# Loading q and k of two batches in token order, and transposing them by DMA

## The chip, the cores and the metric

The kernel runs on one core of a Trainium2 chip. A core has a matrix engine (TensorE, in the profile PE, its weight loads PEld), a vector engine (VectorE, DVE), a scalar engine (ScalarE, ACT), GpSimd (POOL) and SyncE (SP). GpSimd and SyncE only issue DMAs here: the loads from GpSimd, the stores and the DMA transposes from SyncE. The metric is device time of one execution in microseconds (us), lower is better. Three executions of the kernel before took 190.57, 191.4 and 191.51 us, median 191.4 us.

## The reference: what is computed

Attention with a local window of 96 keys and 8 global keys, over 4 batches, 8 heads, 768 tokens and a head dimension of 64, followed by a mixing block over 512 channels:

```python
scores = scale * np.matmul(q, k.transpose(0, 1, 3, 2))
keep = is_global | is_local            # first 8 keys, or 0 <= i - j < 96
scores = np.where(keep, scores + bias, -1e9)
x = softmax(scores) @ v                # then (B, S, 512)
theta = x @ w_theta
y = w_tok_r @ (x * cos(theta)) + w_tok_i @ (x * sin(theta))
u = x + y
out = u + np.maximum(u @ w_ch, 0.0)
```

q, k, v, the weights and the output are float32; the kernel casts its inputs to bfloat16 as they are loaded.

## The kernel before

Tokens are cut into `NT` = 6 tiles of 128, heads into `NP` = 4 pairs of two, so that a pair fills 128 rows (2 heads x 64).

**Loads.** `load_qk` (L69) and `load_v` (L76) issue from GpSimd. q and k come with six neighbouring tokens of a head on one partition, so one run in memory is 6 x 64 numbers (768 bytes as bfloat16). v comes in token order, so a run is 64 numbers (128 bytes). A batch from 1 on is loaded by `load_all` (L364): one DMA for q, one for k, one for v. The tile `qk` has one buffer: q and k of a batch can be loaded only when the last pair of the batch before has been read out of it. `vn` has two.

**Prep** (`prep`, L180), once per batch and pair. VectorE copies q and k of the pair into `qkn`, heads side by side (L189; for the first two pairs of batch 0, ScalarE copies k). TensorE transposes 6 tiles of q and 6 of k against the identity into PSUM (L198, 12 matmuls). VectorE copies q out as `qT` (L203) and ScalarE k as `kT` (L205); these copies also put the tokens back in order. Two VectorE copies build `kG` (L209, L210): the keys of the inner tiles, with the 8 global keys in place of the first 8 of each tile. `qT`, `kT` and `kG` have six buffers each, four of which a batch uses.

**Attention** (`scores` L215, `values` L262): per pair, three steps of score matmuls (L230), an exponential on ScalarE (L234) and a product with a table of biases on VectorE (L242, L245), then the matmuls with v (L278), a reciprocal and a product that give `x_sb` (L286, L288). `xtrans` (L290) transposes `x_sb` into `xT`, by DMA from batch 1 on (L292).

**Mixing**: `theta` (L304) multiplies by `w_theta` (L313), takes cosine and sine on ScalarE (L317, L318) and forms `zri` on VectorE (L321). `mix` (L326) holds the token matmuls (L332), and VectorE adds x to give `u` (L337). `utrans` (L341) transposes `u`, by DMA from batch 1 on (L346) but for the last tile. `chan` (L353) multiplies by `w_ch` (L357), VectorE forms the output tile (L360) and SyncE stores it (L362).

**Order.** Each batch has a head (the last channel matmuls of the batch before, the preps of the next batch and this batch's theta) and a mix phase, into which `weave` (L391) sets the attention of the next batch, step by step. `chan` follows `mix` by two tiles. In batch 0 the preps of batch 1 lie inside the mix phase; the preps of batches 2 and 3 lie in the heads of batches 1 and 2. TensorE's instructions keep the order of the program (`manual_schedule`, L409). On the other engines and on the DMA queues of GpSimd and SyncE a planner orders them when the program is built: among those that its own estimate of time holds to be ready, the earliest in the program first. So an instruction can be set ahead of earlier ones: the load of v for batch 2 stands in the program after those of q and k, but goes at 32.46 us, and q and k at 54.61 us. Where `behind` (L176) is used, an instruction can't be set ahead of the latest token matmul or the latest `u`; the copies into `qkn` and the TensorE transposes are held so. At run time each engine and each queue works strictly in the order it was given.

Of the kernel before, what the change touches and what calls it, by code (L numbers as in the profile page):

```python
# [10 lines left out]
BF = mybir.dt.bfloat16  # L11
# [5 lines left out]
def kernel(  # L17
# [13 lines left out]
    nc = tc.nc  # L31
    B, H, S, D = q.shape
    T = 128
    NT = S // T
    DM = H * D
    NC = DM // T
    NP = H // 2
    NG = int(n_global)
# [8 lines left out]
    ld = ctx.enter_context(tc.tile_pool(name="ld", bufs=2))  # L47
    att = ctx.enter_context(tc.tile_pool(name="att", bufs=2))
# [7 lines left out]
    def ps_small(shape, dtype):  # L56
        return small.tile(shape, dtype, name="ps", tag="ps")

    loads = {}

    def alloc_loads(b):
        qk = ld.tile([T, 2, H, NT, D], BF, name="qk", bufs=1)
        vn = ld.tile([T, H, NT, D + 1], BF, name="vn")
        nc.vector.memset(vn[:, :, :, D:D + 1], 1.0)
        loads[b] = (qk, vn)

    def load_qk(b, h0, n, which=(0, 1)):  # L69
        qk = loads[b][0]  # L70
        for i_ in which:
            nc.gpsimd.dma_start(  # L72
                out=qk[:, i_, h0:h0 + n].rearrange("p h t d -> p h (t d)"),
                in_=(q, k)[i_][b, h0:h0 + n].rearrange("h (p t) d -> p h (t d)", p=T))
# [5 lines left out]


    alloc_loads(0)
    load_qk(0, 0, 2)
    load_qk(0, 2, 2)
    load_v(0, 0, 4)
    load_qk(0, 4, 2)
    load_qk(0, 6, 2)
    load_v(0, 4, 4)
# [76 lines left out]
    def warm(n):  # L165
        ps = ps_small([T, 512], FP)
        for _ in range(n):
            nc.tensor.matmul(ps, lhsT=zero[:, 0:T], rhs=zero, start=True, stop=True)
# [3 lines left out]
    qkT = {}  # L172
# [3 lines left out]
    def behind(eng):  # L176

        return tc.issue_after(anchor[eng]) if eng in anchor else nullcontext()

    def prep(b, p, w=0):  # L180
        qk = loads[b][0]
        if (b, 0) not in qkT:
            x_sb[b] = moe.tile([T, NP, NT, T], BF, name="x_sb", bufs=2)
            xT_sb[b] = moe.tile([T, NC, S], BF, name="xT", bufs=1)

        qkn = att.tile([T, NT, 2, 2, D], BF, name="qkn", bufs=3)
        with behind("dve"):
            for i_ in range(2):
                (nc.scalar.copy if b == 0 and i_ and p < 2 else nc.vector.tensor_copy)(  # L189
                    out=qkn[:, :, i_].rearrange("p t h d -> p h t d"), in_=qk[:, i_, 2 * p:2 * p + 2])  # L190
        qT = att.tile([T, S], BF, name="qT", bufs=6)
        kT = att.tile([T, S], BF, name="kT", bufs=6)
        kG = att.tile([T, NT - 2, T], BF, name="kG", bufs=6)
        for i_, dst in ((0, qT), (1, kT)):
            ps = ps_small([T, NT, T], BF)
            with behind("pe"):
                for t_ in range(NT):
                    nc.tensor.transpose(ps[:, t_, :], qkn[:, t_, i_].rearrange("p h d -> p (h d)"), ident)  # L198

            dst = dst.rearrange("p (n t) -> p n t", t=NT)  # L200
            src = ps.rearrange("p t n -> p n t")
            if i_ == 0:
                nc.vector.tensor_copy(out=dst, in_=src)  # L203
            else:
                nc.scalar.copy(out=dst, in_=src)  # L205
            if w:
                warm(w)

        nc.vector.tensor_copy(out=kG, in_=kT[:, T:(NT - 1) * T].rearrange("p (t n) -> p t n", t=NT - 2))  # L209
        nc.vector.tensor_copy(out=kG[:, :, 0:NG], in_=kT[:, None, 0:NG].to_broadcast([T, NT - 2, NG]))  # L210
        qkT[(b, p)] = (qT, kT, kG)

    ebuf = {}
# [150 lines left out]
    def load_all(b):  # L364
        alloc_loads(b)
        load_qk(b, 0, 8)
        load_v(b, 0, 8)
# [41 lines left out]
    with tc.manual_schedule(engines={mybir.EngineType.PE}):  # L409
        warm(8)  # L410
        prep(0, 0, 4)
        distances()
        bias_table(0)
        for p in range(1, NP + 1):
            if p < NP:
                prep(0, p, 2 if p == 1 else 0)
                bias_table(p)
            if p == 2:
                vglob(0, 0, 4)
            if p == 3:  # L420
                vglob(0, 4, 4)
            for c in range(NT // 2):
                scores(0, p - 1, c)
                if p == 1:
                    warm(1)
            if p > 1:
                values(0, p - 2, 0)
                values(0, p - 2, 1)
            if p > 2:
                xtrans(0, p - 3, nc.scalar.copy)  # L430
        values(0, NP - 1, 0)
        values(0, NP - 1, 1)
        xtrans(0, NP - 2, nc.scalar.copy)
        xtrans(0, NP - 1, nc.scalar.copy)
        trans_w(0, nc.scalar.copy)
    rest = []
    for b in range(B):
# [3 lines left out]
        lag = 2  # L441
        th = [lambda c=c, j=j: theta(b, c, j) for c in range(NT // 2) for j in range(2)]
        pre = [lambda p=p: prep(nxt, p) for p in range(NP)] if nxt else []
        if b == 0:
            order = th
# [61 lines left out]
```

The softmax here doesn't subtract the row's maximum and nothing guards it: scores larger than these inputs give would overflow.

## Time and profile before

| | |
|---|---|
| median of three executions | 191.4 us |
| the profiled execution | 191.4 us |
| its span, first to last instruction | 189.6 us |
| mean granted TensorE clock | 0.973 |
| TensorE busy | 167.9 us, 89% |
| VectorE busy | 137.9 us, 73% |
| ScalarE busy | 102.9 us, 54% |
| packets of GpSimd's load queue | 35760 |
| packets of SyncE's queue | 22304 |

Busy times of TensorE overlap, since matmuls are pipelined and their ends are modelled: twelve transposes that follow each other have 0.22 us each in the profile, and the next group starts some 0.7 us after their first. So TensorE's cost is read from starts. Lines of the profile name a source line (L198), an engine, an operation, the tile written and the tiles read, how often, and then the busy time and the mean of one. Batches are numbered 0 to 3; "(2, 0)" is pair 0 of batch 2, and for `u` it is the tile of tokens.

### The profile page before, as it was taken

To read this page: it belongs to the slowest core of one execution; us is meant where nothing else is said; L and a number is where in the kernel's file an instruction comes from. 1 tells how busy PE (TensorE), PEld (TensorE's weight loads), DVE (VectorE), ACT (ScalarE), POOL (GpSimd) and SP (SyncE) were. 2 spreads that over 40 slices of the span, in tenths; PEclk is the share of its full clock that TensorE was granted. 3 is DMA by queue.
4 is the path that set the end of the run, shared out by engine and by line. 5 is a ranking of instruction groups with operands and counts; after the bars stand their busy time and mean duration, and the time that the engine had idled before them with its cause. 6 is when DMAs were issued, how large, how long until landed. Compare 5 with 4: busy or idle time off the path is not lost.

```text
span 189.6 us, 3693 instructions
## 1 busy us (share of the span) xinstructions
PE 167.9 (89%) x1500; PEld 89.1 (47%) x1523; DVE 137.9 (73%) x309; ACT 102.9 (54%) x122; POOL 27.1 (14%) x31
## 2 busy tenths in 40 slices
PE   7855787899999999999939999999999999999981
PEld 2424665445656555654414454644454544434430
DVE  5839987386999997998853786998877864734422
ACT  2469988871397684598724360499663604800010
POOL 7974361300040004020000000000000000000000
PEclk9999669999999999999987999999999999999999
DMA  4999999999999983999991337301165374113432
GB/s 63 153 188 181 210 209 207 204 189 142 130 83 182 225 116 75 148 142 146 223 116 58 74 91 185 109 3 55 28 66 141 88 145 148 59 32 107 118 106 111
DMA packets 58081, 23.97 MB, mean 126 GB/s; under 512 B 44240, under 2 KB 54992, under 8 KB 58064
## 3 DMA queue, kind: packets, MB, share of 16 engines
q0 software_dynamic: 35760, 12.85, 70.6%
q1 hardware_dynamic: 22304, 10.88, 25.0%
q8 instruction: 12, 0.20, 0.5%
q14 instruction: 5, 0.04, 0.1%
HBM read 25.69 MB, written 6.29 MB: 169 GB/s over the span
## 4 chain that ended last, share of the span: by engine, by line
PE 55%; ACT 14%; DVE 13%; DMA 12%; issue 2%; POOL 2%; ACTq 0%; POOLq 0%
PE ps L332 22%; PE ps L357 10%; DMA uT<-u 8%; PE pb L313 7%; ACT e L234 6%; PE pb L230 5%; DMA vn<-in_v_dram 4%; PE pb L278 4%; DVE qT L203 4%; ACT cs L317 3%; PE ps L198 3%; DVE qkn L189 2%; PE ps L278 2%; DVE zri L321 2%; POOL qk L72 2%
## 5 line engine op out<-in xcount | busy, mean ns | idle before, releaser
L234 ACT ACTIVATE e<-pb 128x1024 bf16<-128x1024 f32 (+1 forms) x48 | 44.1, 958 | 25.8 <-PE pb L230 25.7
L332 PE MATMUL ps<-zri,w_tokT_111 128*128 128x512 bf16 x141 | 53.6, 381 | 0.9 <-issue 0.3
L332 PE MATMUL ps<-zri,w_tokT_110 128*128 128x512 bf16 x130 | 49.5, 382 | 1.3 <-DVE zri L321 0.8
L337 DVE TENSOR_TENSOR u<-x_sb,ps 128x512 bf16<-128x512 bf16 x24 | 16.5, 687 | 16.6 <-PE ps L332 16.0
L357 PE MATMUL ps<-w_ch_bf,uT 128*128 128x512 bf16 x94 | 25.3, 391 | 3.7 <-DMA uT<-u 3.5
L360 DVE SCALAR_TENSOR_TENSOR o_sb<-ps,u 128x512 f32<-128x512 f32 x24 | 16.5, 687 | 11.4 <-PE ps L357 11.4
L313 PE MATMUL pb<-w_theta_bf,xT 128*128 128x512 bf16 x93 | 23.6, 379 | 0.7 <-ACT xT L299 0.4
L321 DVE TENSOR_TENSOR zri<-x_sb,cs 128x512 bf16<-128x512 bf16 x48 | 18.3, 421 | 7.2 <-ACT cs L317 6.1
L242 DVE TENSOR_TENSOR e<-e,etab 128x1024 bf16<-128x1024 bf16 (+1 forms) x32 | 19.7, 617 | 3.5 <-ACT e L234 3.5
L230 PE MATMUL pb<-qT,kT 64*128 64x128 bf16 x224 | 17.9, 231 | 4.7 <-ACT e L234 4.6
L332 PEld LDWEIGHTS <-w_tokT_110 128*128 128x128 bf16 x144 | 14.1, 98 | 15.2 <-issue 1.1
L332 PEld LDWEIGHTS <-w_tokT_111 128*128 128x128 bf16 x144 | 14.1, 98 | 13.2 <-issue 0.5
L205 ACT COPY kT<-ps 128x768 bf16<-128x768 bf16 x16 | 12.9, 805 | 13.4 <-PE ps L198 13.4
L230 PEld LDWEIGHTS <-kT 64*128 64x128 bf16 x224 | 10.0, 99 | 18.3 <-issue 16.7
L351 ACT COPY uT<-ps 128x512 bf16<-128x512 bf16 x7 | 4.1, 587 | 26.1 <-PE ps L350 26.1
L317 ACT ACTIVATE cs<-pb,halfpi 128x1024 bf16<-128x1024 f32 x12 | 13.4, 1120 | 8.9 <-issue 6.8
L278 PEld LDWEIGHTS <-e 128*128 128x128 bf16 x352 | 14.7, 100 | 6.8 <-issue 1.0
L198 PE MATMUL ps<-ident,qkn 128*128 128x128 bf16 x192 | 16.1, 232 | 1.1 <-DVE qkn L189 0.9
L198 PEld LDWEIGHTS <-qkn 128*128 128x128 bf16 x192 | 12.8, 103 | 8.4 <-DVE qkn L189 6.1
L230 PE MATMUL pb<-qT,kG 64*128 64x128 bf16 x128 | 13.6, 228 | 2.0 <-DVE kG L210 2.0
L203 DVE COPY qT<-ps 128x768 bf16<-128x768 bf16 x16 | 15.2, 947 | 0.0
L357 PEld LDWEIGHTS <-uT 128*128 128x128 bf16 x96 | 8.4, 99 | 13.5 <-DMA uT<-u 4.7
(63 smaller groups left out, 204.3 us busy)
## 6 DMA issues: line engine op xcount, KB each, us to landing
out_dram<-o_sb SPq DMA_DIRECT2D x24, 256.0 KB, 2.3
qk<-in_q_dram POOLq DMA_DIRECT2D x3, 768.0 KB, 8.1
qk<-in_k_dram POOLq DMA_DIRECT2D x3, 768.0 KB, 13.6
vn<-in_v_dram POOLq DMA_DIRECT2D x3, 768.0 KB, 22.7
w_nat<-in_moe_w_tok_r_dram POOLq DMA_DIRECT2D x3, 384.0 KB, 13.6
w_nat<-in_moe_w_tok_i_dram POOLq DMA_DIRECT2D x3, 384.0 KB, 14.8
qk<-in_q_dram POOLq DMA_DIRECT2D x4, 192.0 KB, 6.4
qk<-in_k_dram POOLq DMA_DIRECT2D x4, 192.0 KB, 6.7
```

The lines of the kernel that those rows point to most:

```text
L198: nc.tensor.transpose(ps[:, t_, :], qkn[:, t_, i_].rearrange("p h d -> p (h d)"), ident)
L203: nc.vector.tensor_copy(out=dst, in_=src)
L230: nc.tensor.matmul(pb[:, hh, o:o + T], lhsT=lhsT, rhs=qT[R, (own, nxt)[part]], start=True, stop=True)
L234: ins = nc.scalar.activation(e_c, pb[:, :, 0:n], AF.Exp, scale=scale).ins
L242: nc.vector.tensor_mul(e_c, e_c, tab[:, :, s0:s0 + n // T].rearrange("p a s n -> p a (s n)"))
L278: nc.tensor.matmul(o, lhsT=l_, rhs=r_, start=(i_ == 0), stop=(i_ == len(mms) - 1))
L313: nc.tensor.matmul(pb[:, j, :], lhsT=xT[:, dc, st * T:(st + 1) * T], rhs=w_theta_bf[:, dc, :], start=(dc == 0), stop=(dc == NC - 1))
L317: nc.scalar.activation(cs[:, 0], pb, AF.Sin, bias=halfpi)
L321: nc.vector.tensor_mul(zri[b][:, i_, 2 * c + j_, :].rearrange("p (g d) -> p g d", g=NP), xb[:, :, 2 * c + j_, :], cs[:, i_, j_].rearrange( ...
L332: anchor["pe"] = nc.tensor.matmul(ps, lhsT=w_tokT[wi][:, st, tt * T:(tt + 1) * T], rhs=zri[b][:, wi, st, :], start=(st == 0 and wi == 0), ...
L337: anchor["dve"] = nc.vector.tensor_add(u_sb[b, tt].rearrange("p (g d) -> p g d", g=NP), x_sb[b][:, :, tt, :], ps.rearrange("p (g d) -> p g ...
L357: nc.tensor.matmul(ps_c, lhsT=uT[:, dc, :], rhs=w_ch_bf[:, dc, :], start=(dc == 0), stop=(dc == NC - 1))
```

## The change

For batches 2 and 3, q and k are loaded one head at a time in token order, with the two heads of a pair side by side, and the pair is transposed straight from the loaded tile by two DMAs of SyncE. The `qkn` copies, TensorE transposes and PSUM copies of these two batches are gone. Batches 0 and 1 go as before. The two copies that build `kG` have become the function `global_keys`; their number and their form are the same. The way called `"dma"` is in the code and no batch takes it.

```diff
+    way = ["pe", "pe", "natural", "natural"]

     def alloc_loads(b):
-        qk = ld.tile([T, 2, H, NT, D], BF, name="qk", bufs=1)
+        if way[b] == "natural":
+            qk = ld.tile([T, 2, NP, NT, 2, D], BF, name="qk", bufs=1)
+        else:
+            qk = ld.tile([T, 2, H, NT, D], BF, name="qk", bufs=1)
...
     def load_qk(b, h0, n, which=(0, 1)):
         qk = loads[b][0]
+        if way[b] == "natural":
+            for h in range(h0, h0 + n):
+                for i_ in which:
+                    nc.gpsimd.dma_start(out=qk[:, i_, h // 2, :, h % 2, :],
+                                        in_=(q, k)[i_][b, h].rearrange("(t p) d -> p t d", p=T))
+            return
...
+    def global_keys(kT, kG):
+
+        nc.vector.tensor_copy(out=kG, in_=kT[:, T:(NT - 1) * T].rearrange("p (t n) -> p t n", t=NT - 2))
+        nc.vector.tensor_copy(out=kG[:, :, 0:NG], in_=kT[:, None, 0:NG].to_broadcast([T, NT - 2, NG]))
+
     def prep(b, p, w=0):
...
+        if way[b] == "natural":
+            for i_, dst in ((0, qT), (1, kT)):
+                nc.sync.dma_start_transpose(out=dst.rearrange("p (t n) -> p t n", t=NT),
+                                            in_=qk[:, i_, p].rearrange("p t h d -> p (t h d)"))
+            global_keys(kT, kG)
+            qkT[(b, p)] = (qT, kT, kG)
+            return
```

`behind` is not around the new DMA transposes nor around `global_keys`. The new branch of `prep` returns ahead of the `qkn` copies, the transposes and the PSUM copies.

More of the change, by code (lines that the diff above doesn't have):

```diff
@@ L184, in prep @@
             xT_sb[b] = moe.tile([T, NC, S], BF, name="xT", bufs=1)
+        qT = att.tile([T, S], BF, name="qT", bufs=6)
+        kT = att.tile([T, S], BF, name="kT", bufs=6)
+        kG = att.tile([T, NT - 2, T], BF, name="kG", bufs=6)
+        if way[b] == "natural":
[5 more added lines that the diff above has]
+            return
         qkn = att.tile([T, NT, 2, 2, D], BF, name="qkn", bufs=3)
@@ L190, in prep @@
                     out=qkn[:, :, i_].rearrange("p t h d -> p h t d"), in_=qk[:, i_, 2 * p:2 * p + 2])
-        qT = att.tile([T, S], BF, name="qT", bufs=6)
-        kT = att.tile([T, S], BF, name="kT", bufs=6)
-        kG = att.tile([T, NT - 2, T], BF, name="kG", bufs=6)
+        if way[b] == "dma":
+            tr = att.tile([T, NT, 2, T], BF, name="tr", bufs=2)
+            nc.sync.dma_start_transpose(out=tr.rearrange("p t i n -> p (t i) n"),
+                                        in_=qkn.rearrange("p t i h d -> p (t i h d)"))
         for i_, dst in ((0, qT), (1, kT)):
+            if way[b] == "dma":
+                (nc.scalar.copy if i_ else nc.vector.tensor_copy)(
+                    out=dst.rearrange("p (n t) -> p n t", t=NT),
+                    in_=tr[:, :, i_].rearrange("p t n -> p n t"))
+                continue
             ps = ps_small([T, NT, T], BF)
@@ L207, in prep @@
                 warm(w)
-        nc.vector.tensor_copy(out=kG, in_=kT[:, T:(NT - 1) * T].rearrange("p (t n) -> p t n", t=NT - 2))
-        nc.vector.tensor_copy(out=kG[:, :, 0:NG], in_=kT[:, None, 0:NG].to_broadcast([T, NT - 2, NG]))
+        global_keys(kT, kG)
         qkT[(b, p)] = (qT, kT, kG)
```

## The prediction

> **What bounds the kernel now.** I read the totals first, then the heads of batches 1 and 2 by stretches of time, the chain of waits there, and last the DMA queues with the landing times of single transfers.
>
> The first part of the page, then the answer for three stretches (busy us and count of PE, PEld, DVE, ACT and POOL, then TensorE's clock, the DMA share and GB/s):
>
> ```profile
> PE 167.9 (89%) x1500; PEld 89.1 (47%) x1523; DVE 137.9 (73%) x309; ACT 102.9 (54%) x122; POOL 27.1 (14%) x31
> ```
> ```profile
> 75.40:90.00 14.60, 14.38 (x113) 7.42 (x114) 13.65 (x36) 11.55 (x13) 1.86 (x3) 1.00 1.36 147
> 90.00:98.80 8.80, 5.40 (x63) 2.73 (x64) 6.45 (x12) 4.58 (x6) 0.00 (x0) 0.98 1.13 166
> ...
> 118.80:131.00 12.20, 11.97 (x101) 6.51 (x103) 11.89 (x33) 9.79 (x11) 0.00 (x0) 1.00 0.17 56
> ```
>
> TensorE is the bound nearly everywhere, and in the two heads (75.4 to 90 and 118.8 to 131) VectorE is as full. These hold the preps of batches 2 and 3. Between them lies the one stretch with a real hole, 90 to 98.8. The chain of waits there:
>
> ```profile
> 90.08 8.61 DMA uT<-u
> 98.69 0.05 issue
> 98.74 1.89 PE ps L357 x4
> ```
>
> The first transpose of u of batch 1 lands 8.61 us after issue. TensorE stands 2.90 us for it (95.84 to 98.74) and restarts slowly: four channel matmuls take 1.89 where elsewhere they take 0.86. The hole costs 2.9 + 1.0 = 3.9. Why it lands late shows in the DMA part, the last number being us to landing:
>
> ```profile
> qk<-in_q_dram POOLq DMA_DIRECT2D x1, 768.0 KB, 8.1
> qk<-in_k_dram POOLq DMA_DIRECT2D x1, 768.0 KB, 13.6
> ...
> uT<-u SPq DMA_TRANSPOSE x17, 2.4
> xT<-x_sb SPq DMA_TRANSPOSE x12, 2.8
> ```
>
> q and k of batch 3 (issued 83.98 and 84.85) fill the DMA engines until 98.4. A transpose that lands in 2.4 otherwise comes home when they end.
>
> **What the Trainium skill says.** "DMA: Bandwidth & Descriptors", section "Issuing engines are not separate DMA queues": DMAs of SyncE and GpSimd run on the same 16 engines and interleave. The trace agrees: 2.4 against 8.61. The same page, "Why small descriptors are slow (HBM only)", gives short pieces a fixed overhead, 27% at 256 bytes. The trace has the price for this very pattern, below. "Advanced Engine Details and Errata", section "X-Bar Transpose (TRN2)": transposing DMAs are as fast as ordinary ones. The trace: 2.8 for a transpose of 192 KB, 2.3 for a store of 256 KB; near enough.
>
> **What goes.** Per batch 48 TensorE transposes; six have 0.35 from their start to the next group's (76.39 to 76.74), so 48 x 0.058 = 2.8. VectorE loses 8 qkn copies, 2.64 in the first head (row L189), and 4 qT copies, 3.80 (row L203): 6.4. ScalarE loses 4 kT copies, 3.25. What is saved must be followed through each head, since theta needs xT:
>
> Batch 1: xT of pair 3 is issued at 73.89 and lands 2.76 later, 76.65; theta starts at 76.74 now, so not much sooner. Theta is 24 matmuls of 0.216, with four of chan (0.86) after the third group of four. Steps c=0, 1, 2 end at 78.4, 81.0, 82.7 without transposes. The mix then starts at 82.7, against 85.59. ScalarE's pairs (2.0 to 2.1 a step) end at 80.5, 83.0 and 85.0, its table load (1.28) at 86.3; the first exponential follows, against 89.18. Both say 2.9 sooner.
>
> Batch 2: xT lands at 118.51; the three steps end at 120.2, 122.8, 124.5. Mix at 124.5 against 127.78, exponential at 128.2 against 131.37: 3.2 sooner. The second head has DMA traffic of 0.17, nothing hidden.
>
> Together 2.9 + 3.2 = 6.1. The rest of the 12.8 of VectorE and 6.5 of ScalarE lies beside TensorE.
>
> **What comes: loads.** Per batch 12,288 packets of 128 bytes in place of 2,048 of 768. The two v loads issued at 25.73 and 32.46 have this form: behind a full queue they land at 49.17 and 55.15, k of batch 1 ahead of them at 42.85. So 12,288 small packets took 55.15 - 42.85 = 12.3; the old q and k of batch 1 in the same queue 42.85 - 35.10 = 7.75. The load is 4.6 longer per batch when the queue is full. Issue: GpSimd takes 0.75 for a DMA of 256 packets and 1.46 for 3,072, so about 0.88 for 768, and 16 x 0.88 = 14.1 in place of 1.75. Batch 2's loads start when prep (1, 3) has been read, 54.61 as now, and end near 54.61 + 14.1 + 3.5 = 72 (3.5 is what the program's first load takes, issued at 1.25 and landed at 4.7), against 67.24. Their first reader stood at 75.98, so 4 to spare, and pair 0 is in by 62. Nothing else waits behind them on GpSimd's queue before v of batch 3 at 73.30. The cost is nothing; without that cover it is the 4.6.
>
> **What comes: transposes.** 16 more on SyncE, 1.21 of its queue each, 9.7 per batch, and 768 packets each. Ahead of 75 the queue has long idle stretches, and in 98.8 to 118.8 it issues 9 transposes and 5 stores, about 13 of 20. What stands behind a waiting transpose is the next uT (for chan), xT (for theta) and the stores. In the steady part uT lands at 107.33 and chan takes it at 110.70: 3.4 to spare, so one pair ahead (2.4) costs nothing and two (4.8) cost 1.4. Nothing in the old trace shows their order; I bound this from 0 to 4, and take 1.
>
> **What moves: batch 3's load and the hole.** The load of batch 3 waits for the last transpose of batch 2 rather than for a qkn copy at 83. If the transposes are set early, that is about 73; if in program order, 75.2 + 8 x 1.21 + 2.8 = 88. In the first case v (issued 73.30, landing 85.8) and q and k share the queue until 85.8 + 12.3 = 98; in the second until 88 + 14.1 = 102. Either way the first uT, now issued near 87.2 and wanted near 92.9, flies through full engines. Under v's small packets a store issued at 77.01 took 6.73 in place of 2.3; under k 8.61. So it lands at 93.9 to 95.8, the hole is 1.0 to 2.9, plus 1.0 restart: 2.0 to 3.9 against 3.9. Waiting to 98 would be 6.1 + 1.0, 3.2 worse; landing undisturbed 3.9 better. I take a gain of 1.0, which the queueing above uses up.
>
> The sum: 189.6 - 6.1 + 1.0 - 1.0 = 183.5 of span; the profiled execution is 191.4, 1.8 more than its span, so 185.3. It equals the median shown.
>
> **Rivals.**
>
> *The hole closes.* Small packets let transposes through, as the 8.61 came under long ones. Against it: the store of 6.73 under v. It gives 185.3 - 3.9 = 181.4.
>
> *The gain is eaten on DMA.* uT waits for the whole queue (3.2 more) and pairs of prep transposes stand ahead of others (up to 3 more): 188.5 to 191.5, middle 190. For it: 98.69 fell just after the load's end. Against: the load of small packets leaves more turns.
>
> *Slower: kG of batch 3 blocks VectorE.* Its copies are no longer behind a TensorE transpose that `behind` holds, and the planner may set them where it believes kT to be there. If v goes ahead of q and k, v lands at 85.8, the four loads of pair 0 at 85.8 + 12.3 / 4 = 88.9, their transposes through full engines (6.3, as xT at 63.13) at 95. A copy set ahead of batch 1's first u (87.2) then holds VectorE for 8 to 10, and with it zri, u and the products with the biases; TensorE has four PSUM banks for mix and chan and must stop. It decides against the change where the wait is over 6.1 and what VectorE's free time takes up (1 to 2). With 9 to 10 in place it gives 185.3 + 9.7 = 195, with the same for batch 2 up to 200. For it: the planner sets instructions early (v of batch 2 at 32.46, ahead of q and k), and a queue of several loads is where an estimate errs most. Against: in the kernel before no VectorE instruction stands for a DMA after the first load of v (3.5) and q (0.9), but there loads had 20 us of lead.
>
> That the change doesn't do what it says: the folding of global keys is in both kernels unchanged, so that part is worth zero, and is no case of its own.
>
> **How the numbers follow.** Forecast 0.38 (own range 183 to 188), hole closes 0.12, eaten 0.13, slower 0.37. A measurement tells 0.5% from no change, 1 us: faster is below 190.4, slower above 192.4. Forecast and first rival are faster, of the second 0.05, so 0.55; 0.08 same; 0.37 slower. For the range, half of the first rival lies below 181 (0.06) and a quarter of the slower above 199 (0.09): 181 to 199 leaves 0.15. I call faster the likeliest since every TensorE microsecond removed sits in a stretch where it is 98% busy, while the loss needs an order that the page doesn't show.
>
> **What would show it.** SyncE 16 transposes of qT and kT; load queue 35760 - 4096 + 24576 plus 16 for each of 28 more DMAs = 56,688 packets; no L198, L203 or L205 work after 55. First mix of batch 1 near 82.7 and of batch 2 some 6 ahead of 127.8. GpSimd 16 issues near 0.88. The hole of the first uT 1 to 3. Wrong it is where a kG copy shows idle VectorE ahead of it with a DMA of kT as releaser, where theta waits for xT behind prep transposes, or where SyncE stands for qk with u waiting behind.

## The result and the profile after

| | before | after |
|---|---|---|
| median of four executions | 191.2 us (190.57 to 191.51) | 215.0 us (213.41 to 216.86) |
| ratio, 95% interval | | 1.122 [1.114, 1.131] |
| profiled execution, its span | 191.4, 189.6 us | 215.6, 213.8 us |
| mean granted TensorE clock | 0.973 | 0.912 |

The kernel became 12% slower. The forecast was 185.3, with 199 as its upper end. Medians in this text are over all executions of a kernel; ratios leave out those that took over 1.5% more than its fastest. The totals on the page of the kernel after, and the clock row of its 40 slices (5.3 us each, in tenths of full speed):

```profile
PE 167.4 (78%) x1405; PEld 86.7 (41%) x1427; DVE 128.4 (60%) x285; ACT 97.4 (46%) x114; POOL 49.8 (23%) x59
...
PEclk9995799999999658965559999999999999999999
```

The copies that are gone had 12.6 us on VectorE and 6.5 on ScalarE, as forecast; the totals, in which neighbouring instructions overlap, fall by 9.5 and 5.5. TensorE's sum barely moves, though 95 of its instructions are gone: theta's matmuls have a mean of 413 ns, before 379, in stretches with a low clock. What grew is idle time, and the row shows where: slices 14 to 21 (69 to 112 us), where the clock falls to 0.5. To place it, I cut each trace at the first token matmul of each batch, so that a stretch holds the mix phase of a batch and the head of the next:

| stretch, us | before | after | difference |
|---|---|---|---|
| start to the first mix of batch 0 | 37.11 | 37.54 | +0.43 |
| to the first mix of batch 1 | 48.48 | 77.33 | +28.85 |
| to the first mix of batch 2 | 42.19 | 37.27 | -4.92 |
| to the first mix of batch 3 | 35.09 | 34.72 | -0.37 |
| to the end | 26.76 | 26.95 | +0.19 |

The sum is 24.2, the difference of the spans. So nearly 29 are lost before batch 1 is mixed, and 5 come back later. Three pieces of the lossy stretch, by windows of the kernel after (length, then busy us and count of PE, PEld, DVE, ACT, POOL, then clock, DMA share and GB/s):

```profile
54.00:75.00 21.00, 12.28 (x158) 7.01 (x161) 10.71 (x22) 10.68 (x13) 13.65 (x16) 0.92 1.60 137
75.00:82.00 7.00, 4.59 (x55) 3.55 (x55) 4.67 (x13) 2.05 (x2) 0.00 (x0) 0.52 1.01 180
82.00:107.00 25.00, 9.29 (x68) 4.11 (x68) 7.67 (x19) 3.97 (x6) 15.34 (x17) 0.70 1.78 136
```

Every computing engine stands most of the last 25 us. TensorE has three long holes in the stretch; its waits from 60 to 115 us (us in total, times, longest):

```profile
PE pb L260 <- DVE x_sb L318: 10.6, 1, 10.6
PE ps L380 <- DVE u L367: 10.4, 1, 10.4
...
PE pb L343 <- DMA xT<-x_sb: 4.8, 1, 4.8
```

They are 25.8 of the 28.9. The costliest groups name the reason. In the kernel after, L193 is the first copy of `global_keys`, L343 the theta matmuls (the last field is idle time ahead of the group and its releaser); then its chain of waits around 77 to 110 (start, us, what):

```profile
L343 PE MATMUL pb<-w_theta_bf,xT 128*128 128x512 bf16 x95 | 25.4, 413 | 5.3 <-DMA xT<-x_sb 4.8
L193 DVE COPY kG<-kT 128x512 bf16<-128x512 bf16 x16 | 4.9, 306 | 31.9 <-DMA kT<-qk 31.9
```
```profile
76.95 4.33 DMA kT<-qk
...
90.15 6.15 DMA kT<-qk
...
96.30 10.22 DMA xT<-x_sb
...
106.57 4.02 PE pb L343 x9
```

VectorE stood 31.9 us ahead of kG copies whose kT was still in the air, in seven waits. Five lie before batch 1's mix: batch 2's keys at 68.70, 75.33 and 81.31 (4.18, 6.33, 2.00), in the middle of batch 0's mix phase, and batch 3's at 98.78 and 103.68 (11.03, 3.81), before batch 1 had even its theta. Behind these copies stood u and the products of the softmax. TensorE's first hole ends at 77.41, when an `x_sb` behind batch 2's second kG copy is there, and its second at 99.93, when a u behind batch 3's first one is there. The third is SyncE's: the transposes of batch 3's first two pairs, waiting for their load, had been put ahead of xT of batch 1's last pair. Its `x_sb` was ready at 87.16; the xT was issued at 96.30 and landed 10.22 later at 106.52, theta from 106.57.

The loads themselves did what was forecast. The queue's 56,688 packets are the number foreseen, one issue cost 0.863 for q and 0.906 for k, batch 2's loads were issued from 55.00 to 67.72 and landed by 75.52. But their readers no longer start at 75.98: the transposes on SyncE follow the loads closely, the first at 61.51, and wait for them (the last line, of SyncE's waits, is for both batches):

```profile
q0 software_dynamic: 56688, 12.85, 77.5%
...
qk<-in_q_dram POOLq DMA_DIRECT2D x16, 96.0 KB, 5.5
```
```profile
SPq L206 <- DMA qk<-in_q_dram: 19.1, 5, 10.6
```

What did not stay as it was is the flight of a transposing DMA. The DMA answer for 68 to 97 us of the kernel after (last number: median us to landing), where one transpose alone takes 2.75:

```profile
kT<-qk SPq DMA_TRANSPOSE x5, 8.4
qT<-qk SPq DMA_TRANSPOSE x4, 6.3
xT<-x_sb SPq DMA_TRANSPOSE x4, 5.4
```

### The profile page after: what moved, and what is told of

Read it like the earlier page. It is cut to its first block, busy times and chain, and to the rows that moved or that the text cites. A ratio compares the mean times of both kernels' runs of the same rounds, so it can differ in the third digit from the quotient of the medians.

```text
span 213.8 us, 3553 instructions
## 1 busy us (share of the span) xinstructions
PE 167.4 (78%) x1405; PEld 86.7 (41%) x1427; DVE 128.4 (60%) x285; ACT 97.4 (46%) x114; POOL 49.8 (23%) x59
## 3 DMA queue, kind: packets, MB, share of 16 engines
q0 software_dynamic: 56688, 12.85, 77.5%
## 4 chain that ended last, share of the span: by engine, by line
PE 39%; DMA 24%; DVE 13%; ACT 11%; POOL 6%; SPq 4%; issue 2%; ACTq 0%; DVEq 0%; POOLq 0%
PE ps L362 14%; PE pb L343 10%; DMA kT<-qk 8%; PE ps L387 7%; DMA xT<-x_sb 5%; POOL qk L79 4%; ACT e L264 4%; DMA vn<-in_v_dram 4%; DMA uT<-u 3%; DMA qk<-in_k_dram 3%; SPq L206 3%; PE pb L260 3%; ACT cs L347 2%; PE pb L308 2%; DVE u L367 2%
## 5 line engine op out<-in xcount | busy, mean ns | idle before, releaser
L264 ACT ACTIVATE e<-pb 128x1024 bf16<-128x1024 f32 (+1 forms) x48 | 44.2, 957 | 35.7 <-PE pb L260 35.6
L343 PE MATMUL pb<-w_theta_bf,xT 128*128 128x512 bf16 x95 | 25.4, 413 | 5.3 <-DMA xT<-x_sb 4.8
L347 ACT ACTIVATE cs<-pb,halfpi 128x1024 bf16<-128x1024 f32 x12 | 13.4, 1116 | 24.9 <-issue 12.9
L367 DVE TENSOR_TENSOR u<-x_sb,ps 128x512 bf16<-128x512 bf16 x24 | 16.5, 686 | 12.7 <-PE ps L362 12.6
L193 DVE COPY kG<-kT 128x512 bf16<-128x512 bf16 x16 | 4.9, 306 | 31.9 <-DMA kT<-qk 31.9
L79 POOL DMA_DIRECT2D qk<-in_q_dram x16 | 13.8, 863 | 33.5 <-DVE qkn L215 19.9
L308 PEld LDWEIGHTS <-e 128*128 128x128 bf16 x352 | 15.5, 102 | 8.0 <-issue 1.9
L343 PEld LDWEIGHTS <-xT 128*128 128x128 bf16 x96 | 9.6, 104 | 18.3 <-DMA xT<-x_sb 5.7
L79 POOL DMA_DIRECT2D qk<-in_k_dram x16 | 14.5, 906 | 0.0
L308 PE MATMUL pb<-vn,e 128*128 128x65 bf16 x168 | 12.8, 197 | 1.0 <-DVE e L272 0.4
```

The source lines that it names most:

```text
L79: nc.gpsimd.dma_start(out=qk[:, i_, h // 2, :, h % 2, :], in_=(q, k)[i_][b, h].rearrange("(t p) d -> p t d", p=T))
L264: ins = nc.scalar.activation(e_c, pb[:, :, 0:n], AF.Exp, scale=scale).ins
L308: nc.tensor.matmul(o, lhsT=l_, rhs=r_, start=(i_ == 0), stop=(i_ == len(mms) - 1))
L343: nc.tensor.matmul(pb[:, j, :], lhsT=xT[:, dc, st * T:(st + 1) * T], rhs=w_theta_bf[:, dc, :], start=(dc == 0), stop=(dc == NC - 1))
L347: nc.scalar.activation(cs[:, 0], pb, AF.Sin, bias=halfpi)
L367: anchor["dve"] = nc.vector.tensor_add(u_sb[b, tt].rearrange("p (g d) -> p g d", g=NP), x_sb[b][:, :, tt, :], ps.rearrange("p (g d) -> p g ...
```

## The experiments

Three causes were in question: the place of the kG copies on VectorE, the place of the transposes on SyncE, and the DMA engines that transposes share with loads. Line numbers are those of each kernel. The stretches above are used throughout, those of before being 48.48 and 42.19 for the two that matter. Where no ratio with its interval is at hand, the spread of the runs is given.

**e1, kG held on VectorE.**

```diff
-            global_keys(kT, kG)
+            with behind("dve"):
+                global_keys(kT, kG)
```

> The two kG copies of batches 2 and 3 are held behind the latest u on VectorE; SyncE's order stays that of the changed kernel. Theory O (the order: VectorE stands up to 31.9 us for kT because the copies were set ahead of their data, and SyncE holds xT behind transposes that wait for loads): VectorE's waits for kT fall under 6 us, what SyncE does to xT remains, 194 to 204 us. Theory S (SyncE's queue alone decides, VectorE's waits only show it): 210 to 216 us. Theory D (the loads in short runs and the 16 transposes are more than the DMA engines can do in time, the waits only move): 208 to 216 us, with TensorE standing for kG or kT.

Measured: 212.35 us, ratio 1.103 [1.093, 1.113]. What VectorE waits for kT and TensorE for xT:

```profile
PE pb L344 <- DMA xT<-x_sb: 27.2, 4, 12.6
...
DVE kG L193 <- DMA kT<-qk: 3.7, 3, 2.7
```

28 us of kG's waiting are gone, and only 2.7 us of time. The whole stall has moved to theta: xT of batch 1 stands behind the prep transposes on SyncE, and these behind a load. Two instruction streams were blocked by the same late transfers, and freeing one shows the other. The second stretch, though, is 35.30, the shortest of all runs.

**e2, the transposes held on SyncE** (behind the latest xT), kG free.

```diff
-            nc.sync.dma_start_transpose(
+            anchor["sp"] = nc.sync.dma_start_transpose(
...
+            with behind("sp"):
+                for i_, dst in ((0, qT), (1, kT)):
+                    nc.sync.dma_start_transpose(...)
```

> The 16 DMA transposes of q and k are held behind the latest xT transpose on SyncE; the planner then sets the kG copies later by itself. Theory O: waits for kT on VectorE and for xT on TensorE are nearly gone, 185 to 194 us, and if my sum of the heads was right, near 186. Theory S: the same, so this run alone doesn't part O from S. Theory D: the transposes come later still, batch 3's load starts later, 205 us or more.

Measured: 201.75 us, ratio 1.043 [1.032, 1.053]; stretches 52.51 and 47.07. kG comes later here too, as the planner sees the later transposes. But batch 2's eight now run from 76.63 on beside v of batch 3 (issued 73.93, landed 90.85). From e2's chain of waits, SyncE's own time for one transpose:

```profile
86.22 3.82 SPq L207
...
91.74 1.21 SPq L207
...
93.11 2.75 DMA kT<-qk
```

Under v even the issue stretches from 1.21 to 3.82, and the first three land after 9.0 to 11.4. kG still waits 23.0 us, now for transposes that are really late. In the second head they stand one behind the other from 124.18 to 136.54, with no load near, and zri waits behind their kG.

**e5, kG of pairs 1 to 3 at the step ahead of their use**, on e2.

```diff
+            if p:
+                late[(b, p)] = (kT, kG)
+            else:
+                with behind("dve"):
+                    global_keys(kT, kG)
...
+                if p + 2 < NP:
+                    add(0, keys_now, b, p + 2)
```

> As with the transposes held behind xT, and the kG copies of pairs 1 to 3 are issued one scores step ahead of their use and held behind the latest u. Theory O: no wait for kT on VectorE over 1 us, 184 to 190 us, the lowest of the four. Theory S: like the run with the transposes held, within 1 us of it. Theory D: 205 us or more.

Measured: 199.75 us (195.57 to 200.15). kG waits 14.9, down from 23.0. The executions overlap with those of e2 (199.36 to 202.77), so a gain in time is not shown.

**e6, batch 3's v loaded behind its q and k**, on e5.

```diff
+        with behind("pool") if b == B - 1 else nullcontext():
             nc.gpsimd.dma_start(out=vn[...], in_=v[...])
```

> As the run with late kG copies, and v of batch 3 is loaded after q and k of batch 3, so that the 8 transposes of batch 2 meet no load. Theory C (the transposes of batch 2 took 9 to 11 us each because v's short runs filled the DMA engines): the eight are issued within 10 to 11 us in place of 17, each lands in about 2.8, the first head is 5 to 7 us shorter, 191 to 194 us. Theory R (SyncE's own rate of one transpose per 1.2 us is the limit, whatever else is on the engines): within 2 us of the run before it, 196 to 200 us.

Measured: 194.64 us, ratio 1.013 [1.005, 1.021]. Batch 2's transposes now fly alone, 2.75 to 3.9 each, and the first stretch is 45.29: 3.19 shorter than before, where the forecast had 2.9 for this head. The second is 50.98 in the profiled execution, the longest of its four (196.18). Its chain of waits:

```profile
97.24 6.68 DMA uT<-u
...
107.86 8.16 DMA uT<-u
...
118.45 8.24 DMA uT<-u
```

The one buffer of `qk` lets batch 3's load begin only after the last transpose of batch 2 has read it, at 90.06. q, k and v then fly from 90 to 126.5, all through batch 1's mix phase, where these uT take about three times their 2.4.

**e7, the transposes spread over the mix phases**, on e6 (pairs 0 and 1 of batch 2 early, batch 3's between batch 1's attention steps, also behind uT).

```diff
+            for p_ in {1: (0,), 2: (1, 2), 3: (3,)}.get(p, ()) if nb == 3 else ():
+                add(0, trans, nb, p_)
+            if nb == 2 and p < 2:
+                add(0, trans, nb, p, False)
```

> As the run with v last, and the transposes are spread: pairs 0 and 1 of batch 2 as soon as they are loaded, all of batch 3 inside the mix phase of batch 1 behind its xT and uT. If only place and company of the transposes cost time, the heads shrink as forecast, 184 to 189 us. If the DMA transposes are too many for SyncE beside uT and xT wherever they stand, TensorE stands for uT instead, 192 us or more.

Measured: 202.79 us, ratio 1.059 [1.051, 1.067]. Worse at both ends: early transposes make xT late (9.24 to landing), and the others meet the load, where a uT issued at 115.93 lands after 10.09, the longest piece of e7's chain.

**e8, batch 2 alone** (`way = ["pe", "pe", "natural", "pe"]`, the order as in the change).

> The change for batch 2 alone; batch 3 goes the old way. Theory O: the loss splits with the waits of the kG copies, 12.5 us of 31.9 for batch 2 and 19.4 for batch 3, so 198 to 203 us. If batch 2 alone carries it (the transposes delay xT of batch 1): 208 us or more. If batch 3 alone: 188 to 192 us.

Measured: 207.94 us, ratio 1.087 [1.079, 1.095]; first stretch 68.24, second 39.13. Most of the loss (19.8 of 28.9 in the first stretch) is batch 2's own. kG waits 13.4, in batch 0's mix phase, and so batch 1's attention is late and its last xT, issued at 87.58, meets the load of batch 3, though that is made the old way: it lands after 9.71.

**e4, the load alone**: token order from DMA, and TensorE transposes straight from the loaded tile.

```diff
-                nc.sync.dma_start_transpose(...)
+                ps = ps_small([T, NT, T], BF)
+                with behind("pe"):
+                    for t_ in range(NT):
+                        nc.tensor.transpose(ps[:, t_, :], qk[:, i_, p, t_].rearrange("p h d -> p (h d)"), ident)
+                dst = dst.rearrange("p (t n) -> p t n", t=NT)
+                (nc.scalar.copy if i_ else nc.vector.tensor_copy)(out=dst, in_=ps)
```

> q and k of batches 2 and 3 are loaded in token order per head as in the change, but TensorE transposes them straight from the loaded tile, and VectorE and ScalarE copy them out; no qkn copies, no DMA transposes of q and k. Theory O: the load is hidden, VectorE saves 5 us of copies in the heads, 187 to 191 us, 12,288 packets in 13 to 16 us from first issue to last landing. Theory D in its form that the short runs are to blame: 198 us or more, with the load of a batch over 20 us.

Measured: 186.99 us, ratio 0.973 [0.965, 0.981]. Half of the change is a gain. TensorE's wait for uT (before: 2.90 for one):

```profile
PE ps L391 <- DMA uT<-u: 0.3, 1, 0.3
```

The second stretch is 37.76 in place of 42.19, the first 47.97 in place of 48.48. The hole at the first uT of batch 1 is closed: its issue at 90.38 comes home at 96.02 (5.64, where it was 8.61), with q and k of batch 3 still landing until 98.86. With nothing on TensorE changed but what the transposes read, the second stretch is as short as in the kernel before without any load of batch 3 (37.81, e20 below): its gain of 4.4 is this hole.

**e10, e13, e4 for three and for four batches** (`"natural"` from batch 1 on, or for all).

> Loads in token order with transposes on TensorE, for batch 1 too. If the load of batch 1 is hidden as well, 184 to 187 us (eight qkn copies fewer in the mix phase of batch 0). If it comes too late, since its queue is full until 55 us and short runs take 4.6 us longer there, 189 us or more.

> Loads in token order with transposes on TensorE for all four batches. The start waits for the first pair: four short loads of 768 packets in place of two of 256, some 2 to 4 us later, against four copies less on VectorE and ScalarE. If the start outweighs, 186 to 190 us; if not, 183 to 185.5 us.

Measured: e10 185.75 us, ratio 0.969 [0.963, 0.974], the fastest version with all its loads; the first stretch is 47.33. e13 191.8 us, ratio 1.010 [0.998, 1.023]: its first stretch is 52.06, 3.6 longer than before, which costs what the rest gains. In it VectorE stands 2.08 for v of batch 1, and TensorE 2.07 behind it; what the rest is stays open.

**e11 and e12, long runs**: e11 is the change, and e12 is e6, with q and k in pieces of 768 bytes by pair. The tokens come out in another order, so the attention of batches 2 and 3 is over mixed tokens; the work is the same.

```diff
-            for h in range(h0, h0 + n):
+            for h in range(h0, h0 + n, 2):
...
-                    nc.gpsimd.dma_start(out=qk[:, i_, h // 2, :, h % 2, :],
-                                        in_=(q, k)[i_][b, h].rearrange("(t p) d -> p t d", p=T))
+                    nc.gpsimd.dma_start(
+                        out=qk[:, i_, h:h + 2].rearrange("p h t d -> p h (t d)"),
+                        in_=(q, k)[i_][b, h:h + 2].rearrange("h (p t) d -> p h (t d)", p=T))
```

> The changed kernel, but q and k of batches 2 and 3 come by pairs in long runs (768 bytes as bfloat16, 256 packets for a DMA) in place of short ones; the same 16 DMA transposes read the tile as it lies, so that tokens and heads of q and k are mixed up and the scores of these batches are not the reference's. Theory D (short runs under the transposes are to blame): kT lands in time, 192 to 200 us. Theory O (the order alone): the planner sets kG and the transposes as early as before and they wait as long, 208 to 216 us.

> The run with transposes held, late kG copies and v last, but with q and k in long runs as in the run before (q and k mixed up in the same way). If short runs are what holds uT up in the mix phase of batch 1 (6.7 to 8.2 us to landing there), uT lands in 2.5 to 5 and the time is 185 to 189 us. If any load beside the transposes does it, uT stays over 6 and the time is within 2 us of 194.6.

Measured: e11 208.72 us (205.95 to 210.74), kG waits 25.7. e12 192.62 us, ratio 1.015 [0.998, 1.032]. So short pieces, in sixteen issues a batch in place of eight, are some 6 us of the change's loss in its own order; the larger part is there without them. And a load of long pieces does to the transposes what one of short pieces did. The DMA answer for 90 to 118 us of e12, uT alone being 2.4 and xT 2.75:

```profile
uT<-u SPq DMA_TRANSPOSE x5, 7.2
xT<-x_sb SPq DMA_TRANSPOSE x4, 9.0
```

**e14, e6 with batch 3 the old way.**

> As the run with v last, but batch 3 goes the old way: long loads and TensorE transposes. If the DMA transposes gain what was forecast where no load runs beside them (2.9 us in the head of batch 1) and batch 3's part is what cost the rest: 187 to 190 us, with uT of batch 1 landing late once as in the kernel before. If the transposes cost on their own: 192 us or more.

Measured: 194.39 us, ratio 1.017 [0.977, 1.056], an interval that holds faster as well as slower. The profiled execution, the fastest (191.65), has 45.29 and 45.22: the first head's gain whole, and batch 3's q, k (long pieces again) and v in the air from 90.88 to 117.3, with uT at 7.17, 8.52 and 8.00.

**e19 and e20, batch 3 without a load**: e19 is e5, e20 the kernel before, with batch 3 computed from batch 2's q, k and v.

```diff
-            load_all(b + 2)
+            if b + 2 == B - 1:
+                loads[b + 2] = loads[b + 1]
+            else:
+                load_all(b + 2)
```

> The held transposes with late keys (199.75), and no load for batch 3: its q, k and v are those of batch 2, loaded once, so batch 3's outputs are batch 2's. Nothing of a load is left after 75 us; the 16 DMA transposes stay. If the load of batch 3, which the single buffer of q and k pushes behind the last transpose of batch 2 and into batch 1's mix phase, is what keeps the held orders at 194 to 200: 181 to 185, no transpose of u over 3.5 us to landing, the transposes of batch 2 at 2.7 each. If the transposes themselves hold TensorE (their 1.2 on SyncE ahead of xT, keys waiting): 189 or more, with waits of TensorE for xT or of VectorE for kT of over 5 in all.

> The control for the run beside it: the kernel before, with batch 3 computed from batch 2's q, k and v, which are loaded once (batch 3's outputs are then batch 2's). The hole of 3.9 at the first transpose of u of batch 1 closes, and nothing else: 187 to 188.5. If it stays above 190, the load of batch 3 was not what made that hole.

Measured: e19 185.14 us, ratio 0.963 [0.956, 0.970], 14.6 below e5's median and 10.4 below its fastest execution; e20 187.29 us, ratio 0.976 [0.971, 0.981]. So in the mended order the load of batch 3 (q, k and v) costs 10 us or more, and the hole of before is 4.4 (stretch two 37.81 in place of 42.19; I had read 3.9). Against its control the transposes gain 3.19 in the first stretch (45.29 to 48.48) and lose 0.65 in the second (38.46 to 37.81), where 3.2 were forecast. e19's chain of waits at the end of that stretch:

```profile
112.88 2.69 DMA kT<-qk
115.57 2.50 DMA uT<-u
...
118.12 1.04 PE ps L399 x4
```

Each transpose flies in 2.8, undisturbed. But a kT and a qT go ahead of a uT whose u was ready at 111.78; it is issued at 115.57, and TensorE stands 2.58 for it, since its instructions keep the order of the program.

**e22 and e23, batch 3 alone by DMA on e10**, its transposes held as in e19 (e22) or spread between uT and xT as in e7 (e23).

```diff
-        if way[b] == "natural":
+        if way[b] == "natural" and b < 3:
```

> Batches 1 and 2 as in the version at 185.75 (token-order load, TensorE transposes), and batch 3 alone transposed by DMA, held behind the transposes of x, keys late. Batch 3's load now follows TensorE transposes and has landed by 98, so no load flies beside the 8 DMA transposes. If a transposing DMA is free once no load is near and nothing stands behind it, the stretch from the first mix of batch 1 to that of batch 2 falls from 37.8 to 35.3: 183. But they stand at the end of the mix phase, ahead of the last transposes of u, as in the run without the load of batch 3, where that stretch took 38.5: then 186 to 187. I expect the second.

> The same with the 8 transposes set at steps inside batch 1's mix phase, one pair or two between transposes of u and x that have 3.4 to spare. If the order on SyncE is all that is left, the stretch takes 35.3 to 36.5 in place of 37.8 and the time is 183 to 184.7. If a DMA transpose costs beside mixing whatever its place (late transposes of u), 185.75 or more.

Measured: e22 189.05 us, ratio 0.986 [0.982, 0.990]; e23 192.91 us, ratio 1.006 [1.004, 1.009]. Both are slower than e10 (1.4 of e22's profiled span is a later start of batch 0), and spreading the transposes makes it worse: e23's second stretch is 42.55, e22's 38.27, e10's 37.77. The same part of the second head, windows of e22 and then of e10:

```profile
113.00:121.00 8.00, 4.98 (x24) 2.14 (x23) 2.96 (x7) 2.03 (x2) 0.00 (x0) 1.00 0.70 150
```
```profile
111.00:119.00 8.00, 7.90 (x72) 5.08 (x73) 5.17 (x13) 3.42 (x5) 0.00 (x0) 1.00 0.46 123
```

With TensorE's transposes the engine is busy 7.90 of 8 us, 72 matmuls; without them 4.98, 24 matmuls, and the chain of e22 says what it waits for:

```profile
115.69 2.68 DMA kT<-qk
118.37 2.50 DMA uT<-u
...
120.92 1.04 PE ps L410 x4
```

The old transposes were not pure cost: they filled the time in which the last uT of a batch are in flight. In e23 it is the last but one that is late. Its u is ready at 108.88, but on SyncE a kT, an xT, a store, a qT and a kT go ahead of it; it is issued at 115.39 and lands in 2.45, undisturbed:

```profile
114.08 1.21 SPq L207
...
115.39 2.45 DMA uT<-u
...
117.89 1.87 PE ps L420 x4
119.76 3.44 PE pb L376 x12
```

TensorE stands 4.70 for it (e22: 3.02 for the last uT). And the channel matmuls that need this one stand ahead of all theta matmuls in TensorE's order: batch 2's theta starts 35.6 us after batch 1's first mix, in e22 29.0 after, where the late uT stands behind half of theta. Behind e23's hole the granted clock is 0.51 to 120.0, behind e22's it is 1.00. In e1, which gains most in this stretch, the last of the eight transposes is issued 12.3 after the first mix, in e23 30.1 after. Also e22 and e23 took 36.1 for the third stretch, 1.2 over e10, with TensorE standing 1.2 for a uT that lands after 3.9; why that one flies longer stays open.

**e21, one `qk` tile for each pair**, on e10, so that a pair's load waits for that pair alone.

```diff
-            qk = ld.tile([T, 2, NP, NT, 2, D], BF, name="qk", bufs=1)
+            qk = [ld.tile([T, 2, NT, 2, D], BF, name="qk", bufs=4) for _ in range(NP)]
```

> Token-order loads of batches 1 to 3 with TensorE transposes (185.75), and q and k loaded into one tile for each pair in place of one for all, so the load of a pair of the next batch waits only for the transposes of the same pair. The loads of batch 3 then start some 3 to 6 us sooner, pair by pair, and the first transpose of u of batch 1 flies after them: 183 to 185.5. If the planner or the queue of GpSimd keeps them where they are, the same as 185.75 within 0.7.

Measured: 185.91 us, ratio 0.966 [0.960, 0.973], the same as e10. The load starts 2.9 sooner (77.99 for 80.87) and ends where it did, at 98.5.

No run here has a second buffer for `qk` as a whole, which would let batch 3 load early beside a mended order.

## Why the prediction was wrong

**The step that failed: "What comes: transposes".** It counted 16 x 1.21 of SyncE's queue, bounded the consequence "from 0 to 4", and took 1, since "nothing in the old trace shows their order". What the old trace left open was the larger part of the cost. Its cases, one pair or two ahead of a uT, took the pairs as ready. And the kG copies, which read what these transposes write, have no term in the sum at all. In the run the transposes stood waiting for the load that feeds them, flew two to three times as long beside it (5.8 to 8.7 for the kT in question), and held what came behind: VectorE waited 27.4 for kT before batch 1's mix (4.18 + 6.33 + 2.00 + 11.03 + 3.81), and xT of batch 1's last pair stood 9.1 on SyncE. TensorE's three holes behind these waits are 25.8, in a stretch that grew by 28.9. That these sums come close is no proof, as e1 shows that the two waits hide each other; but e6, e12, e14 and e19, with both orders mended and no load beside batch 2's transposes, all have 45.29.

**"What goes": right for the first head, not for the second.** The first gave 3.19 where 2.9 was forecast (e6, e12, e14, e19). The second gives 2.5 in e1 (35.30 against e20's 37.81), but minus 0.65 in e19 and minus 0.5 in e22. The step followed theta's and ScalarE's ends and took what TensorE did between as pure cost. It left out the uT that fly under those transposes.

**"What comes: loads": right on the loads, not on their reader.** Packets and issue time held, and the landing near 72 came at 75.5, within the 4 to spare before the old first reader at 75.98; with TensorE's transposes in that place (e4) the load costs nothing. In the change the first reader stood at 61.51, and the cover was gone.

**"What moves": the flight put too long, and a gain that the change could not use.** I expected a gain of 1.0 of the hole's 3.9, and rated its closing at 0.12. In e4 it closes (4.4): the uT flies 5.64, where 6.73 to 8.61 were foreseen, and TensorE waits 0.3. In the change itself batch 1's mix began at 114.87, after batch 3's load had landed (q and k at 105.20, v at 111.88), so the stretch lost the hole for that reason: of its minus 4.92, e20 makes 4.4 the hole's.

**The rival "slower" was the right one in part, and placed too late and priced too low.** It named kG copies set too early behind a late load, in batch 3's case ahead of batch 1's first u, at 8 to 10; the measured waits for batch 3 are 11.03 and 3.81. It gave batch 2 only 5 more, where VectorE waited 12.5, and it left SyncE out: xT of batch 1 behind batch 3's transposes is in my list of what would make the forecast wrong, but in no sum. Its evidence "against", that no VectorE instruction of the kernel before stands for a DMA past 3.5, came from loads with 20 us of lead. The old trace has no transpose of q or k beside its own load; in the run one lands in 5 to 9 and not in 2.75. It did hold the hint, a uT of 8.61 and an xT of 6.33; this rival used the second for one pair, and the step that took 1 used neither for the sixteen new transposes.

Slips in the sums, none of which decides the outcome: the 1.0 gained at the hole is in 185.3 already, so its closing gives 182.4 and not 181.4; from 92.9 to 98 is 5.1 and not 6.1, so that wait is 2.2 worse and not 3.2; and SyncE issues 7 transposes and 4 stores from 98.8 to 118.8, about 11 us of 20.

The Trainium skill's "Advanced Engine Details and Errata", section "X-Bar Transpose (TRN2)", which stands beside the price, has transposing DMAs as fast as others. Alone they come near it (2.75 here for 192 KB, 2.3 for a store of 256 KB). Its sentence says nothing of landing times beside other traffic, and I read it as if it did. A row that I passed over bears on the choice itself: "VectorE: DVE Perf Modes", section "Rules for kernel authors", advises TensorE for a 128x128 transpose where its result may go to PSUM. The runs agree in this kernel: 185.75 by TensorE, 189.05 and 192.91 with one batch by DMA.

What stays open: which share of the transposes' delay is queueing behind packets and which is the stretched issue, and how the loss in the change's own order divides between SyncE and VectorE, since each hides the other.

## What to carry to other kernels

When work goes from an engine to a DMA, ask at once who stands behind its waiting instruction on each queue and each in-order engine; if an estimate decides that order when the kernel is built, price the change with the wait in the worst place, since it can be as long as the load, not as the copy. A latency that a removed instruction used to cover comes back as idle time, so follow each transfer that flew beneath it. And take a change apart: the half that loads in token order gains 3% here, and the half that transposes by DMA turns that into a loss of 12% in the order that the planner gave it.

## What the runs showed of the hardware

- A DMA transpose of 192 KB that lands in 2.75 alone took mostly 5 to 11.4 beside a load of GpSimd's queue (the longest in e2). One of 128 KB, uT, that takes 2.4 alone took much longer whether the load's pieces were 128 bytes (e6: 6.68, 8.16, 8.24) or 768 (e12: 7.18, 10.20, 8.94). SyncE's own time for one of 192 KB goes from 1.21 to as much as 4.13 (the xT of 96.30 in the kernel after).
- Behind several of the holes TensorE's granted clock is low, even while TensorE is busy again. In the kernel after it is 0.50 from 106.6 to 111.0, right behind the third hole, 0.81 to 114.9 and 1.00 from there to 120; TensorE is busy for all of the first two stretches. Theta's matmuls of that batch have a mean of 514 ns, those of the next two batches 379. In the kernel before, the 2.3 us behind the hole of 2.90 (98.7 to 101.0) have 0.50 as well, in the same place as the slow restart. But e22's hole of 3.02 is followed by 1.00, so no length of hole that brings it about is shown.
- A load of 12,288 packets of 128 bytes, spread over 16 issues, disturbed the first uT less than the old one of 2,048 long ones in two issues: 5.64 to landing in e4, 5.50 to 5.77 in e10, e21, e22 and e23, 8.61 before. Whether the size of the pieces or the number of issues does it is not shown. Beside v as well (e6) it is about 8.
